# Where a chunked recurrence keeps its decay products, when its inverse begins, and which engine turns the state: a change of order in a fused fp32 kernel

## The chip, the cores and the metric

The kernel runs on one core of one Trainium2 chip. The metric is the device time of one execution in microseconds (us). The core has engines that run side by side and meet at semaphores: TensorE (PE in the profile, its weight loads PEld), VectorE (DVE), ScalarE (ACT), GpSimd (POOL), and a sync engine (SP) that issues most of the DMA transfers; ScalarE issues the others.

## The reference

Two blocks follow each other, all in fp32. The first is a recurrence over 768 tokens for 4 batches of 8 heads, with a state of 40 x 40 per head:

```python
for t in range(S):
    y[:, :, t] = einsum('bhd,bhde->bhe', r_t, state)
    Sa = einsum('bhde,bhe->bhd', state, a_t)
    state = state * w_t[..., None, :] - einsum('bhd,bhe->bhde', Sa, b_t)
    state = state + einsum('bhd,bhe->bhde', v_t, k_t)
```

The second takes the 3072 tokens of 320 channels that come out: `h = x @ w_in` (320 x 2048), `g = h * sigmoid(h)`, `out = g @ w_out` (2048 x 320).

## The kernel before

The 768 tokens are cut into 12 chunks (n = 0 to 11) of 64. Each chunk is handled in two units (m = 0, 1) of two batches. Two chunks, an even and an odd one, make a pair; one inverse serves both, and the second block runs once for a pair. The names that the profile shows are those of the tiles.

**Preparation of a chunk.** `scale` forms the running products W of w along the tokens with a scan on VectorE, and their reciprocals (written over w). GpSimd multiplies a, b and k by them. `scores` multiplies b and a on TensorE (pm), masks the product on VectorE (sb) and sends it to DRAM (md).

```python
def pre(u, md):
    def scale():
        u.W = sb.tile([128, Q, C + 1], F32, name="W", bufs=6)
        R = u.w[:, :, 1 : C + 1]
        ...
        if "pair" in mark and u.n % 2 == 0:
            pin = lambda x: behind(x, mark["row" if u.m == 0 else "across"])
        for be in range(2):
            ...
            pin(nc.vector.tensor_tensor_scan(W, w, one..., 0.0, ALU.mult, ALU.add))
        pin(nc.vector.reciprocal(R, u.W[:, :, 1 : C + 1]))
    ...
    return [scale, scaled, scores, keys] if u.n < 2 else [scale, reciprocals, scaled, rest, scores]
```

`behind(x, y)` only fixes the order: x stands behind y in its engine's queue. `staged(n)` is true for odd chunks above 3: their a is loaded into `stage`, scaled there, and copied into its final tile by `stack`.

**Inverse of a pair.** The masked scores of both chunks come back from DRAM with another layout into the tile `mi` (one buffer). `row` is one multiplication and one reduction on VectorE, each row needs the one before, and there are 31 of them, growing from 1 to 31 x 31 elements per partition. `back` copies the result into mi, from where it goes to DRAM (xd) and returns as XT; `turned` transposes blocks of XT on VectorE, and `first` and `second` merge the blocks with products on TensorE (pq, po).

```python
mark["tiles"] = [sb.tile([128, 2 * SKIP], F32, name="mi"), sb.tile([128, 32 * 32], F32, name="tmp")]
...
def back():
    at = 0
    if N == 32 or hi - lo == 64:
        at = 16
        nc.scalar.copy(out=mi[L, 0:16], in_=turned[L, 0:16])
    x = nc.vector.tensor_copy(out=mi[L, at:32], in_=turned[L, at:32])
    send(queue, xd[L], mi[L])
```

**A chunk's own chain** has six steps: `keys` (transposes pt of b and k), `right` (pr), `solve` (pu, pw with XT), `read` (pl, masked on VectorE into vl), `write` (pgy: the chunk's outputs and the new state GV; VectorE adds, scales by W and forms yx, which ScalarE's queue sends to xs in DRAM), and `turn` (the transposed state GT for the next chunk). For even chunks `turn` is 16 transposes of 32 x 256 on VectorE, for odd ones products with the identity on TensorE (pt<-ident,GV) and copies on ScalarE.

```python
def turn():
    if u.n > 1 and u.n % 2 == 0:
        ... nc.vector.transpose(out=gt[T, :, 32 * e : 32 * e + 32], in_=wide[E, ...]) ...
        return
    ... nc.tensor.matmul(pt..., lhsT=gv[J, j, q], rhs=ident[J, J]) ... nc.scalar.copy(out=gt[R], in_=pt[j][R])
```

**The second block of a pair.** `fetch` brings xs into xt, then 16 steps follow: four `first` (products ph with wi_s and wl_s, activation into gts), four `second` (products po with wo_s), and the same again. They stand in a queue from which `take(k)` puts k steps at the present place of TensorE's order. `weave` mixes two lists of steps evenly.

**The loop over pairs**, for even n from 4 on:

```python
x = prepare(n + 2)
run(merges[1:2] + keys + merges[2:3] + right)
take(1)
run(solve[0:1] + later[0:2] + [x[i] for i in (0, 5, 1, 6) if x])
take(1)
run(solve[1:2] + later[2:3] + [x[i] for i in (2, 7, 3, 8) if x] + read)
take(1)
run([x[i] for i in (4, 9) if x] + write)
each(keyed, n + 1)
take(1)
x = prepare(n + 3)
run([x[i] for i in (0, 2, 5, 7) if x] + turn)
keys, right, solve, read, write, turn = ...              # of chunk n + 1
run(keys + [x[i] for i in (1, 6) if x] + right)
take(1); run(solve[0:1]); take(1)
run(solve[1:2] + [x[i] for i in (4, 9) if x])            # scores of chunk n + 3
rows = invert(n + 3)
run(rows[0:1] + ...); take(1)
x = read + [load vut, take(1)] + write + ...
fetch, more = moe(n, xs)
x += [partial(fetch, 0), partial(queue.extend, more), partial(take, 2)] + turn
weave(x + [partial(take, 1)] * 6, rows[1:36])
```

(The loads are left out here; `merges` and `later` are the steps of the merge.) Chunks 2 and 3 have a passage of their own ahead of the loop, in the same manner.

Of the kernel before, what the change touches and what calls it, by code (L numbers as in the profile page):

```python
# [9 lines left out]
F32 = mybir.dt.float32  # L10
# [31 lines left out]
def kernel(  # L42
# [284 lines left out]
            nc.gpsimd.tensor_copy(out=u.a[J, j], in_=u.stage[J])  # L327

    def pre(u, md):
        def scale():  # L330
            u.W = sb.tile([128, Q, C + 1], F32, name="W", bufs=6)
            R = u.w[:, :, 1 : C + 1]
            pin = partial(in_order, line="vector") if u.n < 2 else lambda x: x
            if "pair" in mark and u.n % 2 == 0:

                pin = lambda x: behind(x, mark["row" if u.m == 0 else "across"])
            for be in range(2):
                W, w = (x[:, P * be : P * be + P].rearrange("p q t -> p (q t)") for x in (u.W, u.w))
                pin(nc.vector.tensor_tensor_scan(W, w, one.rearrange("p q t -> p (q t)"), 0.0, ALU.mult, ALU.add))
            pin(nc.vector.reciprocal(R, u.W[:, :, 1 : C + 1]))  # L340

        def keys():
            R = u.w[:, :, 1 : C + 1]
            nc.gpsimd.tensor_tensor(out=u.kb[:, :, 0], in0=u.kb[:, :, 0], in1=R, op=ALU.mult)
            junk = sb.tile([128, Q, C], mybir.dt.bfloat16, name="junk")
            c = 2 * (NM * u.n + u.m)
            nc.scalar.activation(out=junk, in_=R, func=AF.Square, accum_out=chk[:, c : c + 1])  # L347
            nc.scalar.activation(out=junk, in_=u.W[:, :, 1 : C + 1], func=AF.Square, accum_out=chk[:, c + 1 : c + 2])

        def reciprocals():  # L350
            R = u.w[:, :, 1 : C + 1]
            nc.gpsimd.tensor_tensor(out=u.kb[:, :, 1], in0=u.kb[:, :, 1], in1=R, op=ALU.mult)  # L352

        def rest():
            keys()
            k = NM * u.n + u.m
            for x in [6, 7] if k == 4 else [k + 3]:
                if x < NM * NN:
                    load_w(units[x // NM][x % NM], ([w0] + early)[(x - 4) % 3])

        def scaled():
            if staged(u.n):
                nc.gpsimd.tensor_tensor(out=u.stage, in0=u.stage, in1=u.W[:, :, 0:C], op=ALU.mult)
                return
            for j in range(2):
                J = slice(DP * j, DP * j + DP)
                nc.gpsimd.tensor_tensor(out=u.a[J, j], in0=u.a[J, j], in1=u.W[J, :, 0:C], op=ALU.mult)  # L367
            if u.n < 2:
                R = u.w[:, :, 1 : C + 1]
                nc.gpsimd.tensor_tensor(out=u.kb[:, :, 1], in0=u.kb[:, :, 1], in1=R, op=ALU.mult)  # L370

        def scores():
            if u.m == 0:
                sbs[u.n] = sb.tile([128, NM, 2, P, C], F32, name="sb", bufs=2)
            between(u, sbs[u.n][:, u.m])
            for be in range(2 if u.m == NM - 1 else 0):
                queue = nc.scalar if u.n == 1 or u.n == be == 0 else nc.sync
                for c in range(2):
                    at = 64 * (u.n % 2) + 16 * (2 * be + c)
                    r = C * be + 32 * c  # L380
                    x = send(
                        queue,
                        md[at : at + 16].rearrange("q s t -> s q t"),
                        sbs[u.n][r : r + 32, :, :, :, 32 * c : 32 * c + 32].rearrange("s m j p t -> s (m j p) t"),
                    )
                    if queue is nc.sync:
                        mark["md"] = x.ins
            for x in (4, 5) if u.n == u.m == 1 else ():
                load_w(units[x // NM][x % NM], ([w0] + early)[(x - 4) % 3])

        return [scale, scaled, scores, keys] if u.n < 2 else [scale, reciprocals, scaled, rest, scores]

# [3 lines left out]
    def inverse(md, N, queue, lo=0, hi=128):  # L398
# [38 lines left out]
        def back():  # L437
            turned = XI.rearrange("p t s -> p s t")
            at = 0
            if N == 32 or hi - lo == 64:  # L440
                at = 16
                nc.scalar.copy(out=mi[L, 0:16], in_=turned[L, 0:16])
            x = nc.vector.tensor_copy(out=mi[L, at:32], in_=turned[L, at:32])
            pin(x)
            mark["row"] = x.ins
            send(queue, xd[L], mi[L])
# [163 lines left out]
    def chain(u, xs):  # L610
# [78 lines left out]

        def turn():  # L690

            if u.n > 1 and u.n % 2 == 0:
                wide = GVf[u.m]
                for j in range(2):
                    for e in range(2):
                        for d in range(2):
                            E, T = (slice(DP * j + 32 * x, DP * j + 32 * x + 32) for x in (e, d))
                            at = j * Q * D + 32 * d
                            nc.vector.transpose(
                                out=gt[T, :, 32 * e : 32 * e + 32],  # L700
                                in_=wide[E, at : at + Q * D].rearrange("p (q d) -> p q d", q=Q)[:, :, 0:32],
                            )
                return
            pt = [bank("pt") for _ in range(2)]
            for q in range(Q):
# [203 lines left out]
    def run(steps):  # L909
        for step in steps:  # L910
            step()
# [60 lines left out]
    for u in units[2] + units[3]:  # L972
# [10 lines left out]
    rows = invert(3)  # L983
    weave(
        queue[0:8],
        [x[i] for x in ahead for i in (0, 5, 1, 6, 2, 7, 4, 9, 3, 8)] + [partial(keyed, u) for u in units[2]] + rows[0:19],
        convert[21:31],
    )
    del queue[0:8]
# [29 lines left out]
    take(1)  # L1019
    run(two[0:1] + one_[2:3] + two[1:2] + one_[3:4] + two[2:3] + one_[4:5])  # L1020
    x = prepare(4)
    run(two[3:4] + solve[0:1] + [x[i] for i in (0, 5, 1, 6)] + two[4:5] + solve[1:2] + [x[i] for i in (2, 7, 3, 8)])
    each(keyed, 3)
    run(read)
    each(load_vut, 3)
    take(1)
    run(write + [x[i] for i in (4, 9)])
    each(load_vl, 3)
    x = prepare(5)
    run([x[i] for i in (0, 2, 5, 7)] + turn)  # L1030
    keys, right, solve, read, write, turn = start(3)
    run(keys + [x[i] for i in (1, 6)] + right)
    take(1)
    run(solve[0:1])
    take(1)
    run(solve[1:2] + [x[i] for i in (4, 9)])
    rows = invert(5)
    merges = rows[35:]
    run(rows[0:1] + [x[i] for i in (3, 8)])
    issued["sync"] = mark["mi"]  # L1040
    each(load_v, 4)
    each(load, 6, "bk")
    run(read)
    each(stack, 5)
    x = [partial(each, load_vut, 4), partial(take, 1)]
    x += write + [partial(each, load_vl, 4)] + [partial(keyed, u) for u in units[4]]
    fetch, more = moe(2, xs)
    x += [partial(fetch, 0), partial(queue.extend, more), partial(take, 2)] + turn
    weave(x + [partial(take, 1)] * 8, rows[1:36])
    for n in range(4, NN, 2):  # L1050
        xs = dr.tile([DM, 4 * NM * C], F32, name="xs", bufs=2)
        keys, right, solve, read, write, turn = start(n)
        x = prepare(n + 2)
        later = late.pop(n)
        run(merges[1:2] + keys + merges[2:3] + right)
        each(load_v, n + 1)
        each(load, n + 2, "a")
        each(load, n + 3)
        take(1)
        run(solve[0:1] + later[0:2] + [x[i] for i in (0, 5, 1, 6) if x])  # L1060
        take(1)
        run(solve[1:2] + later[2:3] + [x[i] for i in (2, 7, 3, 8) if x] + read)
        each(load_vut, n + 1)
        take(1)
        run([x[i] for i in (4, 9) if x] + write)
        each(load_vl, n + 1)
        each(keyed, n + 1)
        take(1)
        x = prepare(n + 3)
        run([x[i] for i in (0, 2, 5, 7) if x] + turn)  # L1070
        keys, right, solve, read, write = start(n + 1)[0:5]
        turn = start(n + 1)[5] if n + 2 < NN else []
        run(keys + [x[i] for i in (1, 6) if x] + right)
        each(load_v, n + 2)
        each(load, n + 4, "bk")
        take(1)
        run(solve[0:1])
        take(1)
        run(solve[1:2] + [x[i] for i in (4, 9) if x])
        rows = invert(n + 3)  # L1080
        merges = rows[35:]
        run(rows[0:1] + [x[i] for i in (3, 8) if x])
        take(1)
        if n + 2 < NN:
            each(stack, n + 3)
            x = read + [partial(each, load_vut, n + 2), partial(take, 1)]
            x += write + [partial(each, load_vl, n + 2)] + [partial(keyed, u) for u in units[n + 2]]
            fetch, more = moe(n, xs)
            x += [partial(fetch, 0), partial(queue.extend, more), partial(take, 2)] + turn
            weave(x + [partial(take, 1)] * 6, rows[1:36])  # L1090
        else:
            run(read)
            take(1)
            run(write)
            fetch, more = moe(n, xs)
            fetch(0)
            queue += more
# [155 lines left out]
```

## Time and profile before

| | |
|---|---|
| time, median of 3 | 917.12 us (916.49 to 922.71) |
| span of the profiled execution | 928.1 us |
| TensorE busy | 779.0 us (84%) |
| VectorE busy | 553.2 us (60%) |
| ScalarE busy | 295.8 us (32%) |
| GpSimd busy | 150.9 us (16%) |
| reciprocals of W, VectorE | 24 of 3344 ns |
| turns of GV, VectorE | 80 of 436 ns |
| second block's products ph (wi_s) and po (wo_s), TensorE | 195.8 us and 214.2 us busy |

The page divides the span into 40 equal slices (23.2 us each) and gives the busy share of each engine in tenths; the line PEclk is the clock that TensorE was granted, in tenths of full speed. A group's line names the source line, the engine, the operation, output <- inputs and the shapes, then the busy time and the mean duration of one, then the engine's idle time just before these instructions and what ended most of it. A line of the timeline begins with start and duration in us. Profiled matrix products are counted per pass, two to an fp32 product here. Times in the text without another source are us from the start of the profiled span.

### The profile page before, as it was taken

To read this page: it belongs to the slowest core of one execution; us is meant where nothing else is said; L and a number is where in the kernel's file an instruction comes from. 1 tells how busy PE (TensorE), PEld (TensorE's weight loads), DVE (VectorE), ACT (ScalarE), POOL (GpSimd) and SP (SyncE) were. 2 spreads that over 40 slices of the span, in tenths; PEclk is the share of its full clock that TensorE was granted. 3 is DMA by queue.
4 is the path that set the end of the run, shared out by engine and by line. 5 is a ranking of instruction groups with operands and counts; after the bars stand their busy time and mean duration, and the time that the engine had idled before them with its cause. 6 is when DMAs were issued, how large, how long until landed. Compare 5 with 4: busy or idle time off the path is not lost.

```text
span 928.1 us, 25351 instructions
## 1 busy us (share of the span) xinstructions
PE 779.0 (84%) x10914; PEld 550.9 (59%) x10914; DVE 553.2 (60%) x1084; ACT 295.8 (32%) x688; POOL 150.9 (16%) x156
## 2 busy tenths in 40 slices
PE   2035689998789899999499998599996899996996
PEld 2035587676777557677256767256775366672544
DVE  9989979885376983294973394972577920610000
ACT  2235367543513124231134250125250225220120
POOL 7402033001313101141101140102040000010001
PEclk9665767997599999899799999699998899997999
DMA  7975725654244603537303627212525021212001
GB/s 171 197 145 145 162 75 141 174 140 104 52 87 82 172 2 82 125 67 160 84 23 60 138 65 165 67 43 67 127 57 116 31 46 31 61 23 57 1 1 31
DMA packets 240150, 82.99 MB, mean 89 GB/s; under 512 B 207136, under 2 KB 231968, under 8 KB 240032
## 3 DMA queue, kind: packets, MB, share of 16 engines
q1 hardware_dynamic: 219488, 69.96, 33.8%
q10 hardware_dynamic: 20544, 11.34, 4.8%
q8 instruction: 87, 1.43, 0.6%
q14 instruction: 31, 0.25, 0.1%
HBM read 67.11 MB, written 14.16 MB: 88 GB/s over the span
## 4 chain that ended last, share of the span: by engine, by line
PE 59%; DVE 22%; DMA 10%; issue 3%; ACT 3%; SPq 2%; ACTq 0%; POOLq 0%; DVEq 0%; POOL 0%
PE ph L825 15%; PE po L837 15%; DVE tmp L423 5%; PE pl L268 4%; DVE XI L430 4%; PE ph L830 4%; PE pgy L268 4%; DVE w L340 3%; PE pu L268 3%; PE po L268 3%; PE pt L268 2%; PE pq L268 2%; DMA xs<-yx 2%; PE pr L268 2%; PE pm L268 2%
## 5 line engine op out<-in xcount | busy, mean ns | idle before, releaser
L825 PE MATMUL ph<-xt,wi_s 128*128 128x512 f32 (+1 forms) x448 | 195.8, 584 | 48.1 <-DMA xt<-xs 45.9
L837 PE MATMUL po<-wo_s,gts 128*128 128x320 f32 x768 | 214.2, 436 | 0.0
L837 PEld LDWEIGHTS po<-wo_s,gts 128*128 128x128 f32 x768 | 143.6, 190 | 62.7 <-issue 4.9
L825 PEld LDWEIGHTS ph<-xt,wi_s 128*128 128x128 f32 x448 | 87.7, 206 | 131.8 <-issue 77.3
L832 ACT ACTIVATE gts<-ph 128x512 f32<-128x512 f32 (+1 forms) x112 | 54.3, 534 | 248.8 <-PE ph L830 248.3
L734 DVE TENSOR_TENSOR vl<-pl,ml 128x512 f32<-128x512 f32 x48 | 30.9, 685 | 139.1 <-PE pl L268 81.7
L423 DVE TENSOR_TENSOR tmp<-XI,mi 64x2 f32<-64x2 f32 (+40 forms) x169 | 83.8, 496 | 15.1 <-DMA mi<-md 10.7
L340 DVE RECIPROCAL w<-W 128x512 f32<-128x512 f32 x24 | 80.3, 3344 | 0.9
L430 DVE TENSOR_REDUCE XI<-tmp 64x2 f32<-64x2 f32 (+40 forms) x169 | 76.8, 454 | 4.8
L853 POOL TENSOR_TENSOR ot<-gts,ot 128x320 f32<-128x320 f32 x24 | 20.8, 865 | 282.3 <-ACT gts L851 282.3
L352 POOL TENSOR_TENSOR kb<-kb,w 128x512 f32<-128x512 f32 x20 | 25.3, 1266 | 253.2 <-DVE w L340 157.6
L268 PE MATMUL pm<-a,kb 64*64 64x64 f32 x1280 | 40.1, 235 | 21.9 <-POOL kb L370 15.5
L830 PE MATMUL ph<-xt,wl_s 64*128 64x512 f32 (+1 forms) x224 | 57.9, 594 | 0.0
L268 PE MATMUL pq<-XT,sb 32*32 32x32 f32 (+1 forms) x1280 | 31.0, 207 | 30.8 <-DVE XT L472 15.9
L268 PEld LDWEIGHTS pm<-a,kb 64*64 64x64 f32 x1280 | 36.4, 147 | 27.8 <-POOL kb L370 15.7
L268 PE MATMUL pl<-r,vut 64*128 64x64 f32 x768 | 50.3, 288 | 2.8 <-ACT vl L662 2.3
L268 PEld LDWEIGHTS pl<-r,vut 64*128 64x128 f32 x768 | 48.5, 201 | 5.6 <-ACT vl L662 2.4
L367 POOL TENSOR_TENSOR a<-a,W 64x512 f32<-64x512 f32 x32 | 39.1, 1220 | 66.6 <-PE pq L268 24.0
L347 ACT ACTIVATE junk<-w 128x512 bf16<-128x512 f32 x24 | 15.1, 631 | 105.5 <-DVE w L340 85.0
L268 PEld LDWEIGHTS pq<-XT,sb 32*32 32x32 f32 (+1 forms) x1280 | 27.9, 131 | 35.1 <-issue 18.9
L268 PE MATMUL pt<-ident,kb 128*128 128x128 f32 x192 | 27.9, 304 | 23.4 <-DVE a L312 23.1
L851 ACT COPY gts<-po 128x320 f32<-128x320 f32 x24 | 10.2, 424 | 98.0 <-PE po L837 81.7
(108 smaller groups left out, 1039.9 us busy)
## 6 DMA issues: line engine op xcount, KB each, us to landing
kb<-in_bT SPq DMA_DIRECT2D x48, 128.0 KB
vut<-in_vT SPq DMA_DIRECT2D x48, 128.0 KB
r<-in_rT SPq DMA_DIRECT2D x24, 256.0 KB
w<-in_wT SPq DMA_DIRECT2D x45, 128.0 KB
kb<-in_kT SPq DMA_DIRECT2D x44, 128.0 KB
a<-in_aT SPq DMA_DIRECT2D x32, 128.0 KB
vl<-in_v SPq DMA_DIRECT2D x48, 80.0 KB
xs<-yx ACTq DMA_DIRECT2D x48, 80.0 KB
```

The lines of the kernel that those rows point to most:

```text
L268: x = what(*x, **y)
L340: pin(nc.vector.reciprocal(R, u.W[:, :, 1 : C + 1]))
L352: nc.gpsimd.tensor_tensor(out=u.kb[:, :, 1], in0=u.kb[:, :, 1], in1=R, op=ALU.mult)
L367: nc.gpsimd.tensor_tensor(out=u.a[J, j], in0=u.a[J, j], in1=u.W[J, :, 0:C], op=ALU.mult)
L423: x = nc.vector.tensor_tensor(out=part, in0=X[L, :, t + 1 : N, t + 1 : N], in1=M[L, :, t, t + 1 : N].unsqueeze(2).to_broadcast([hi - lo, I ...
L430: x = nc.vector.tensor_reduce(out=X[L, :, t + 1 : N, t], in_=part, axis=AX.X, op=ALU.add)
L734: nc.vector.tensor_tensor(out=u.vl[:, :, j, D:], in0=pl[j].rearrange("p (q t) -> p q t", q=Q), in1=ml.unsqueeze(1).to_broadcast([128, Q, C ...
L825: in_order(nc.tensor.matmul(ph[n], lhsT=wi_s[:, k, at : at + 128], rhs=xt[:, k, :], start=k == 0, stop=False))
L830: in_order(nc.tensor.matmul(ph[n], lhsT=wl_s[R, i, :], rhs=xt[R, 2, :], start=False, stop=True))
L832: nc.scalar.activation(out=place(2 * i + n)[:, T], in_=ph[n], func=AF.Silu)
L837: in_order(nc.tensor.matmul(po[:, 0:DM], lhsT=place(f)[:, b * 128 : b * 128 + 128], rhs=wo_s[:, NF // 2 * half + f, :], start=f == 0, stop ...
L853: nc.gpsimd.tensor_tensor(out=ot4, in0=rest, in1=ot4, op=ALU.add)
```

## The change

It does four things.

1. The products W of an odd chunk from 5 on are formed in the tile mi, which the inverse does not use at that time, and GpSimd copies them into a W buffer later (`kept`). So the preparation of chunk n + 3 no longer needs a free W buffer and moves ahead of chunk n's `write`.
2. The rows of the inverse stand behind the even chunk's write: the whole chain of the odd chunk, from `keys` on, is now woven with the rows, where before only `read` and `write` were.
3. VectorE turns the state of odd chunks, too (from 5 on); the turn of an odd chunk is held back until the next pair. `back` copies wholly on VectorE.
4. In the passage of chunks 2 and 3 fewer steps of the second block are taken, so that five steps of a pair stand ahead of the next pair's first chunk. Of the other eleven, three come between the odd write and the first step on the next xt, so that TensorE has work while y travels through xs to xt.

```diff
     def pre(u, md):
+        def kept():
+            u.W = sb.tile([128, Q, C + 1], F32, name="W", bufs=6)
+            nc.gpsimd.tensor_copy(out=u.W, in_=u.Wt)
+
         def scale():
-            u.W = sb.tile([128, Q, C + 1], F32, name="W", bufs=6)
+            if staged(u.n):
+                if u.m == 0:
+                    mark["Wt"] = sb.tile([128, 2 * SKIP], F32, name="mi")
+                u.Wt = mark["Wt"][:, Q * (C + 1) * u.m : Q * (C + 1) * (u.m + 1)].rearrange(...)
+            else:
+                u.W = u.Wt = sb.tile([128, Q, C + 1], F32, name="W", bufs=6)
             ...
-            if "pair" in mark and u.n % 2 == 0:
-                pin = lambda x: behind(x, mark["row" if u.m == 0 else "across"])
+            if "pair" in mark:
+                pin = lambda x: behind(x, mark["row" if u.m == u.n % 2 == 0 else "across"])
...
-            if N == 32 or hi - lo == 64:
+            if hi - lo == 64:
                 at = 16
                 nc.scalar.copy(out=mi[L, 0:16], in_=turned[L, 0:16])
...
-            if u.n > 1 and u.n % 2 == 0:
+            if u.n > 1 and u.n != 3:
...  # the loop; the passage before it is changed in the same way and ends with 5 instead of 8 single takes
-        x = prepare(n + 2)
+        x, y = prepare(n + 2), prepare(n + 3)
...
-        run(solve[1:2] + later[2:3] + [x[i] for i in (2, 7, 3, 8) if x] + read)
+        run(solve[1:2] + later[2:3] + [x[i] for i in (2, 8, 3, 9) if x])
+        run([y[i] for i in (0, 6, 1, 7, 2, 8) if y] + held + read)
...
-        run([x[i] for i in (4, 9) if x] + write)
+        run([x[i] for i in (4, 10) if x] + write + [y[i] for i in (5, 11) if y])
         each(load_vl, n + 1)
         each(keyed, n + 1)
         take(1)
-        x = prepare(n + 3)
-        run([x[i] for i in (0, 2, 5, 7) if x] + turn)
-        ...
-        run(keys + [x[i] for i in (1, 6) if x] + right)
-        each(load_v, n + 2)
-        each(load, n + 4, "bk")
-        take(1)
-        run(solve[0:1])
-        take(1)
-        run(solve[1:2] + [x[i] for i in (4, 9) if x])
+        run([y[i] for i in (4, 10) if y])
         rows = invert(n + 3)
-        run(rows[0:1] + [x[i] for i in (3, 8) if x])
-        take(1)
+        run(rows[0:1])
+        run([y[i] for i in (3, 9) if y])
+        x = turn
+        keys, right, solve, read, write = start(n + 1)[0:5]
+        held = start(n + 1)[5] if n + 2 < NN else []
+        x = x + keys + right + [partial(each, load_v, n + 2), partial(each, load, n + 4, "bk")]
+        x += [partial(take, 1), solve[0], partial(take, 1), solve[1], partial(take, 1)]
         if n + 2 < NN:
-            each(stack, n + 3)
-            x = read + [partial(each, load_vut, n + 2), partial(take, 1)]
+            x += [partial(each, stack, n + 3)]
+            x += read + [partial(each, load_vut, n + 2), partial(take, 1)]
             x += write + [partial(each, load_vl, n + 2)] + [partial(keyed, u) for u in units[n + 2]]
             fetch, more = moe(n, xs)
-            x += [partial(fetch, 0), partial(queue.extend, more), partial(take, 2)] + turn
+            x += [partial(fetch, 0), partial(queue.extend, more), partial(take, 2)]
             weave(x + [partial(take, 1)] * 6, rows[1:36])
```

In the order of instructions that results, an even chunk has S S S between its products, then F F F F and one S stand among the odd chunk's, S S S behind the odd write, and F F F F S ahead of the next pair (F and S are the second block's `first` and `second`).

## The prediction

> **What bounds the kernel now.** The second block's work on a pair of chunks comes in two kinds of step: F reads xt (four 128x512 products with wi_s, two with wl_s, two activations), S reads gts (eight products with wo_s). A pair has 8 F and 8 S, in the order F F F F S S S S twice, and from chunk 4 on every pair goes through the same order of work. First view: the page's slices and its groups.
>
> ```profile
> PE   2035689998789899999499998599996899996996
> PEclk9665767997599999899799999699998899997999
> L825 PE MATMUL ph<-xt,wi_s 128*128 128x512 f32 (+1 forms) x448 | 195.8, 584 | 48.1 <-DMA xt<-xs 45.9
> ```
>
> TensorE is busy from the first third on, but a dip comes back every fifth or sixth slice, and PEclk dips with it. The group that waits there is the first F of a pair, for xt: 45.9 us in 5 waits. Second view: the stretch from chunk 6's first merge product (494.6) to chunk 8's (630.6), cut where chunk 7's write ends.
>
> ```profile
> 495.00:574.00 79.00, 77.88 (x1341) 57.28 (x1336) 35.73 (x74) 29.54 (x69) 20.29 (x20) 1.00 0.50 107
> 574.00:630.00 56.00, 43.06 (x251) 24.55 (x246) 47.86 (x79) 10.31 (x20) 2.74 (x2) 0.85 0.27 64
> ```
>
> Columns: stretch, length, busy TensorE, weight loads, VectorE, ScalarE, GpSimd, clock, DMA. In the first stretch TensorE is full and VectorE idles more than half; in the second VectorE is nearly full (the rows of the inverse) and TensorE has a hole and a clock of 0.85. Third view, the order of time, TensorE:
>
> ```profile
> 577.61 1.97 PE L268 MATMUL pm<-a,kb 64*64 64x64 f32 x32 [2.06 <-DVE yx L782]
> 590.46 5.77 PE L825 MATMUL ph<-xt,wi_s 128*128 128x512 f32 x8 [10.88 <-DMA xt<-xs]
> 597.22 3.70 PE L825 MATMUL ph<-xt,wi_s 128*128 128x512 f32 x8
> 601.91 1.98 PE L268 MATMUL pt<-ident,GV 64*40 64x64 f32 x64
> 613.21 17.49 PE L837 MATMUL po<-wo_s,gts 128*128 128x320 f32 x64
> 630.63 1.20 PE L268 MATMUL pq<-XT,sb 32*32 32x32 f32 x64
> ```
>
> (A count of 8 is four products.) Nothing of this pair can be multiplied until both its chunks' y have gone through xs to xt, and nothing of the pair before is left: 10.88 us idle, then the first F at 5.77 for 3.70. VectorE:
>
> ```profile
> 519.02 1.29 DVE L734 TENSOR_TENSOR vl<-pl,ml 128x512 f32<-128x512 f32 x2 [22.67 <-ACT XT L568]
> 571.40 0.16 DVE L423 TENSOR_TENSOR tmp<-XI,mi 128x1 f32<-128x1 f32 x1 [5.36 <-DMA mi<-md]
> 616.77 1.16 DVE L430 TENSOR_REDUCE XI<-tmp 128x31 f32<-128x961 f32 x1
> 624.04 0.70 DVE L472 STREAM_TRANSPOSE XT<-XT 32x512 f32<-32x512 f32 x1 [6.11 <-DMA XT<-xd]
> ```
>
> The rows start at 571.4 and end at 617.9, and XT is turned at 624 to 632, just when TensorE ends its last S (630.6). So both chains close together: filling TensorE alone would bring nothing, the rows have to start earlier too. Why they start so late, the sync queue shows; the scores of chunk 9, which these rows invert, were masked by 557.3:
>
> ```profile
> 555.40 2.05 SPq L221 DMA_DIRECT2D kb<-in_bT  x2
> 562.90 3.18 SPq L221 DMA_DIRECT2D md<-sb  x4
> ```
>
> md is issued behind eight kb loads and two output writes.
>
> **What the skill says.** "TensorE: Matmul & The Clock Gate", What's actually happening: after an idle window of some 3.4 us the array's clock is halved, and is given back after about as long a busy time. The trace agrees (5.77 against 3.70 after 10.88 us idle; 1.00 where TensorE is full). "Perfetto Trace Analysis", Optimization Strategy: where the contended engine changes over time, interleave the regimes. That is this change; the two stretches above are such regimes. "PSUM — Partial Sum Buffer", Engine vs sequencer instructions: ScalarE, VectorE and GpSimd queues are strict FIFO. The trace agrees: VectorE idles 22.67 us before vl with scans of later chunks ready behind it. "VectorE: DVE Perf Modes", The three transpose paths: VectorE turns 32x32 blocks only; here 16 instructions per chunk at 436 ns each.
>
> **The change, part by part.**
>
> *Rows begin behind the even write.* Scans and reciprocals of the odd chunk n+3 move from behind write(n) into VectorE's idle time before vl: 4 scans at 0.74 and 2 reciprocals at 3.34, 9.6 us. With them go the held turn of chunk n-1 (16 x 0.436 = 7.0) and XT's second half: about 18 us into 22.7, so no cost. W has 6 buffers, two a chunk, and chunk n's are read until write(n); hence the products stay in mi and GpSimd copies them to W afterwards (2 copies, an estimate of 1.2 us each from its 128x512 operations at 1.27, beside other work). Now take chunk n's first merge product as t = 0, with durations of this trace: pq, pt, po, pr 7.3; S 4.5; pu/pw and pq 2.9; S 4.5; pu/pw and po 2.9; pl 3.7; S 4.5; pm 2.0; write(n) 5.4 (ends 37.8); pm 2.0; F 4.7; pm of chunk n+3 to t = 46.6. VectorE then has write(n)'s updates, 8.9 from 35.2 (as from 529.3 to 538.2 before), 9 turns (4.0) and the masks, which stand between turns: t = 50. In the sync queue md and mi now follow the vl and r loads, ahead of kb. From the first md issue to mi's landing it took 7.75 before (426.66 to 434.41), so rows start at t = 58. Before it was 571.4 - 494.6 = 76.8: 19 us earlier.
>
> *TensorE's order.* Five steps (F F F F S) of a pair come before the next pair and eleven in it, so that S S S stand between the odd write and the first F. From t = 46.6: pt and pr 3.9, F, pu/pw, F, pu/pw, F, pl 3.7, S: 76; write(n+1) to 81.4; pm 83.4; S S S 13.1 to 96.5. I add 1.8 for pt, whose banks of PSUM are freed by masks that stand behind nine turns: 98.3. Rows: the first 20 take 14.0 (sum of their groups), t = 72; vl at 72 to 75.2; up to row 25 6.7, to 81.9; updates of write(n+1), the last yx at 90. From there to the first F it took 6.4 to 7.8 (715.2 to 721.6; 582.7 to 590.5), so xt is there at t = 97 to 98. TensorE comes at 98.3: the gap closes, with nothing to spare. F F F F S bring 23.2: the next pair starts at 121.5. The last rows end at 90 + 1.4 + 12.5 = 104, copy 1.1, xd and XT 5.0, turned by t = 112: nine us of slack.
>
> *Turns.* 64 products, 1.92 us, leave TensorE in three pairs, and 2.4 us of copies leave ScalarE; VectorE takes 7.0 where it idles.
>
> *Sum.* A pair's work on TensorE without gap: 81.8 (494.6 to 576.4) + 4 x 4.69 + 17.42 = 118.0, and with the 1.8 for pt 119.8; I take 120. Before: from 356.05 to 494.59, 630.63 and 762.76 are 138.5, 136.0 and 132.1. Saved 18.5 + 16.0 + 12.1 = 46.6 us. The start of chunk 4 comes earlier by the three S that now follow chunk 4 instead: there the two small F and two S stand before chunk 3's pl as before, the pm of chunks 4 and 5 have moved ahead, so pl ends near 293.7 (292.0 before), the last yx, now behind row 20, comes at about 308 as before, the first F at 318, and 18.8 + 4.5 + 2 for the slow clock lead to 343 instead of 356. The rows, from about 280 on, are through by 329 and XT by 335, so they don't bind. Those 13.1 us are paid back in the last pair, where they fill its hole: 72.6 up to the last write, S S S 13.1, then 79.6 from the first F to the end at full clock (81.7 less 2.1) and 1 for pt: 166 against 165.3. Total 343 + 3 x 120 + 166 = 869 of the profile's 928.1, a ratio of 0.936; of 917.12 that is 859 us.
>
> **Rivals.** (1) *The gap stays, since xt follows the rows.* The y updates of the odd write stand in VectorE's queue behind row 25. If mi comes late (its buffer is now freed by GpSimd's copies and ScalarE's squares, too), each us puts off xt by a us beyond the one TensorE can cover: 6 us later would mean a pair of 125 and 873 us. For it: the margin of zero above. Against: the copies can start at t = 41, mi lands at 58. (2) *VectorE's added work delays vl or the write of the even chunk.* A scan of mi stands between two vl, waiting for a w load late in the sync queue (I put it at t = 22 to 26, vl at 24). Five us there would be five in each of four pairs: 880. Against it: S and pm still lie between pl and write, 6.5 us. (3) *VectorE becomes the bound.* Its busy time was 83.6 of 135 in a pair; with 7.0 more turns it is 91 of 120. There is slack unless its waits are badly placed; then a pair lasts about 130 and the time is near 890. (4) *Better than thought*: no stall of pt and a clock of 1.00 throughout give 118 a pair, and 852.
>
> **Range and chances.** Most of the gain is work already done at full clock in the first stretch, with a filling that the order of instructions shows; what is unsure is whether waits of 2 to 5 us a pair come in. Predicted 859 us, 8 times in 10 between 847 and 880. Faster by over 2% means under 898.8, so some 40 of the 58 us would have to be lost for it to fail: 0.95. Within 2% 0.04, slower 0.01.
>
> **What the changed profile would show.** The wait of ph for xt falls from 45.9 us to some 10, most of it before chunk 4. pq of chunks 6, 8 and 10 start some 120 us apart, with first rows near t = 58 and clock near 1.00 throughout the pair. Before XT's transposes VectorE idles, or they end well before pq. Turned blocks number 128 and no pt<-ident,GV follows chunk 3. I am wrong if rows start past t = 65, if ph still waits over 5 us in each pair, if vl waits for a scan behind w, or if POOL's copy W<-mi ends after the md issue.

## The result and the profile after

The changed kernel takes 883.09 us (median of 4 runs, 881.11 to 885.63) where the kernel before, run beside it, took 919.09: a ratio of 0.9607, 95% interval 0.9558 to 0.9657. A second comparison gave 0.9626 (0.9597 to 0.9655). Faster, as predicted, but not by as much: 859 was the prediction, 847 to 880 its range.

The page after has a span of 879.6 us instead of 928.1; TensorE is busy 762.4 us of it (87%), VectorE 583.5 (66%). First the slices of TensorE and of its granted clock, and the group that had waited for xt:

```profile
PE   2134688999689999989989989999899999999996
...
PEclk9665868999569999999999999999999999999998
...
L839 PE MATMUL ph<-xt,wi_s 128*128 128x512 f32 (+1 forms) x448 | 185.7, 558 | 6.1 <-ACT gts L846 4.1
```

The dips that came back in every pair are gone, from TensorE and from its clock. Of 45.9 us of waiting for xt nothing is left, and a product takes 558 ns in the mean instead of 584. What remains is 6.1 us, most of it for an activation (gts).

The pairs, from the first pq of chunk 4, 6 and 8 to the next pair's (columns as in the prediction: length, busy TensorE, weight loads, VectorE, ScalarE, GpSimd, clock, DMA):

```profile
340.97:467.35 126.38, 119.75 (x1538) 80.53 (x1537) 98.81 (x164) 39.11 (x90) 27.98 (x26) 0.97 0.42 95
467.35:591.11 123.76, 117.92 (x1538) 79.99 (x1537) 91.22 (x164) 37.29 (x84) 25.87 (x24) 0.99 0.43 97
591.11:712.06 120.95, 118.07 (x1541) 80.48 (x1542) 83.84 (x171) 33.90 (x74) 19.57 (x20) 0.99 0.37 84
```

They were 138.5, 136.0 and 132.1; I had put them at 120 each. Where the second pair's 123.76 us go is seen in the order of time, TensorE first:

```profile
498.47 1.14 PE L268 MATMUL pgy<-r,GT 64*64 64x64 f32 x30 [0.91 <-DVE sb L290]
...
515.61 2.82 PE L268 MATMUL pt<-ident,kb 128*128 128x128 f32 x12 [3.38 <-DVE sb L290]
...
553.30 13.19 PE L851 MATMUL po<-wo_s,gts 128*128 128x320 f32 x48
566.33 3.60 PE L839 MATMUL ph<-xt,wi_s 128*128 128x512 f32 x8
...
578.94 1.98 PE L839 MATMUL ph<-xt,wi_s 128*128 128x512 f32 x4 [1.35 <-ACT gts L846]
...
591.11 1.07 PE L268 MATMUL pq<-XT,sb 32*32 32x32 f32 x56
```

S S S run from 553.30 on, and the first F follows at once at 566.33, taking 3.60 instead of 5.77. The square brackets hold what is left: three waits, of which two are for the masks sb. VectorE's order of the same pair:

```profile
493.60 0.70 DVE L350 TENSOR_TENSOR_SCAN mi<-w,one 128x260 f32<-128x260 f32 x1 [0.56 <-DMA w<-in_wT]
494.22 0.67 DVE L748 TENSOR_TENSOR vl<-pl,ml 128x512 f32<-128x512 f32 x1
494.80 3.34 DVE L351 RECIPROCAL w<-mi 128x512 f32<-128x512 f32 x1
498.06 1.35 DVE L290 TENSOR_TENSOR sb<-pm,ms 128x256 f32<-128x256 f32 x4
...
511.07 4.03 DVE L710 STREAM_TRANSPOSE GT<-GV 32x256 f32<-32x256 f32 x9
515.13 0.76 DVE L290 TENSOR_TENSOR sb<-pm,ms 128x256 f32<-128x256 f32 x2
515.91 0.43 DVE L710 STREAM_TRANSPOSE GT<-GV 32x256 f32<-32x256 f32 x1
516.38 0.76 DVE L290 TENSOR_TENSOR sb<-pm,ms 128x256 f32<-128x256 f32 x2
...
524.32 0.16 DVE L434 TENSOR_TENSOR tmp<-XI,mi 128x1 f32<-128x1 f32 x1 [4.90 <-DMA mi<-md]
...
539.38 1.29 DVE L748 TENSOR_TENSOR vl<-pl,ml 128x512 f32<-128x512 f32 x2 [2.07 <-PE pl L268]
...
577.07 0.70 DVE L483 STREAM_TRANSPOSE XT<-XT 32x512 f32<-32x512 f32 x1 [0.18 <-DMA XT<-xd]
```

A reciprocal of 3.34 us stands right ahead of the first masks, and nine transposes, 4.03 us, right ahead of the second. The rows start at 524.32, 57.0 us into the pair (76.8 before), and the first blocks of XT are turned at 577, 14 us ahead of pq. The masks also hold up the sync queue, whose order is:

```profile
508.85 0.40 SPq L221 DMA_DIRECT2D r<-in_rT  x1
517.16 2.06 SPq L221 DMA_DIRECT2D md<-sb  x4
519.32 2.12 SPq L221 DMA_DIRECT2D mi<-md  x2
```

md goes out as the last mask ends (516.38 + 0.76); the kb loads no longer stand ahead of it.

### The profile page after: what moved, and what is told of

The parts are those of the page before. It is cut to its first block, busy times and chain, and to the rows that moved or that the text cites. A ratio compares the mean times of both kernels' runs of the same rounds, so it can differ in the third digit from the quotient of the medians.

```text
span 879.6 us, 24987 instructions
## 1 busy us (share of the span) xinstructions
PE 762.4 (87%) x10722; PEld 541.6 (62%) x10722; DVE 583.5 (66%) x1132; ACT 286.3 (33%) x672; POOL 159.3 (18%) x164
## 4 chain that ended last, share of the span: by engine, by line
PE 50%; DVE 33%; DMA 7%; issue 3%; SPq 2%; ACT 2%; POOL 1%; ACTq 0%; POOLq 0%; DVEq 0%
PE ph L839 14%; PE po L851 12%; DVE tmp L434 6%; DVE XI L441 5%; DVE w L351 5%; PE ph L844 4%; PE pl L268 3%; PE pt L268 3%; PE po L268 3%; PE pgy L268 2%; SPq L221 2%; PE pr L268 2%; PE pq L268 2%; PE pu L268 2%; DVE GV L787 2%
## 5 line engine op out<-in xcount | busy, mean ns | idle before, releaser
L839 PE MATMUL ph<-xt,wi_s 128*128 128x512 f32 (+1 forms) x448 | 185.7, 558 | 6.1 <-ACT gts L846 4.1
L839 PEld LDWEIGHTS ph<-xt,wi_s 128*128 128x128 f32 x448 | 83.7, 196 | 86.4 <-issue 66.2
L434 DVE TENSOR_TENSOR tmp<-XI,mi 64x2 f32<-64x2 f32 (+40 forms) x169 | 84.6, 501 | 23.6 <-DMA mi<-md 18.7
L867 POOL TENSOR_TENSOR ot<-gts,ot 128x320 f32<-128x320 f32 x24 | 24.4, 1018 | 328.8 <-ACT gts L865 325.4
L441 DVE TENSOR_REDUCE XI<-tmp 64x2 f32<-64x2 f32 (+40 forms) x169 | 76.8, 455 | 5.1
L710 DVE STREAM_TRANSPOSE GT<-GV 32x256 f32<-32x256 f32 x128 | 55.7, 435 | 28.8 <-DMA GV<-in_v 26.9
L268 PE MATMUL pm<-a,kb 64*64 64x64 f32 x1280 | 40.8, 239 | 18.7 <-POOL kb L381 15.5
L351 DVE RECIPROCAL w<-W 128x512 f32<-128x512 f32 x16 | 53.5, 3343 | 0.5
```

The source lines that it names most:

```text
L268: x = what(*x, **y)
L351: pin(nc.vector.reciprocal(R, u.Wt[:, :, 1 : C + 1]))
L434: x = nc.vector.tensor_tensor(out=part, in0=X[L, :, t + 1 : N, t + 1 : N], in1=M[L, :, t, t + 1 : N].unsqueeze(2).to_broadcast([hi - lo, I ...
L441: x = nc.vector.tensor_reduce(out=X[L, :, t + 1 : N, t], in_=part, axis=AX.X, op=ALU.add)
L710: x = nc.vector.transpose(out=gt[T, :, 32 * e : 32 * e + 32], in_=wide[E, at : at + Q * D].rearrange("p (q d) -> p q d", q=Q)[:, :, 0:32],)
L839: in_order(nc.tensor.matmul(ph[n], lhsT=wi_s[:, k, at : at + 128], rhs=xt[:, k, :], start=k == 0, stop=False))
```

## The experiments

**Theory.** The change works as meant, and needs both of its parts; what the prediction missed are waits in in-order queues (masks behind nine turns or a reciprocal, an activation behind a square), each with some clock lost behind it, and a scale taken from one long execution of the kernel before. **Rivals.** The filling with S S S gives nearly all of it; the early rows do; VectorE has become the bound, so that a wait removed comes back elsewhere; the masks' place doesn't matter.

**The kernel before again.** No edit.

> The kernel before, unchanged, profiled once more. The first profile of it has a span of 928.1 us, while its timed runs were 916.5 to 922.7 us. Theory A: the extra 8 to 11 us belong to that one execution; then this profile spans 916 to 921 us, and its pairs of chunks (first pq to first pq) are shorter than 138.5, 136.0 and 132.1 us by some 2 to 3 us each. Theory B: the profile lengthens this kernel each time; then it spans 926 to 930 us with the same pairs, and the ratio that I took to 928.1 was no mistake.

A span of 918.0 us, with pairs of 135.96, 134.74 and 132.73, and chunk 4 starting at 350.04 instead of 356.05. So theory A for the span; of the 10.1 us, 6.0 lie ahead of chunk 4, 3.3 in the pairs and 0.8 in the tail, where I had expected most of it in the pairs. The timed runs of the kernel before went from 916 to 931 us over the comparisons, so the profile of 928.1 shows a long execution; profiling does not lengthen this kernel each time.

**The shift of steps alone** (in the kernel before, the passage ahead of chunk 4):

```diff
-    weave(x + [partial(take, 1)] * 8, rows[1:36])
+    weave(x + [partial(take, 1)] * 5, rows[1:36])
```

> The kernel before with one part of the change alone: five steps ahead of chunk 4, so that S S S stand behind the odd write; rows of the inverse, turns and scans stay where they were. Theory 1 (both chains ended together, so filling TensorE's hole alone brings nothing a pair): pairs of chunks 4, 6 and 8 still last 132 to 137 us, ph's wait for xt nearly vanishes, but the wait of pq for XT (the turned inverse) grows to 8 to 13 us a pair; time 905 to 920 us, that is 0 to 14 below before. Rival (the filling is the gain, the rows hardly matter): pairs 122 to 127 us and 880 to 890 us in all, as the full change.

906.89 us, ratio 0.9832 (0.9783 to 0.9880); pairs of 130.2, 129.1 and 124.3. TensorE's order, from the start of one pair to that of the next:

```profile
479.36 0.31 PE L268 MATMUL pq<-XT,sb 32*32 32x32 f32 x2 [3.42 <-DVE XT L472]
480.50 1.91 PE L268 MATMUL pq<-XT,sb 32*32 32x32 f32 x62 [0.83 <-DVE XT L472]
...
578.34 3.60 PE L825 MATMUL ph<-xt,wi_s 128*128 128x512 f32 x8
...
603.36 1.34 PE L837 MATMUL po<-wo_s,gts 128*128 128x320 f32 x4 [2.87 <-ACT gts L832]
608.43 0.31 PE L268 MATMUL pq<-XT,sb 32*32 32x32 f32 x2 [3.73 <-DVE XT L472]
```

The hole ahead of F is filled, and TensorE now waits for the rows' result XT and for gts, 7 to 8 us a pair (22.8 us for XT in all, 13.0 of them at the start of chunk 4; a pair waits some 4.3 us for XT, where theory 1 had 8 to 13). The time is in theory 1's range, the pairs 2 to 8 us below it: the filling alone does bring something, 6 to 8 us a pair against the second profile of before. In the kernel before the first blocks of XT were turned at 624.0 and 624.9, and pq ran at 630.6: the rows' chain had 5 to 6 us of slack, and that is what this edit takes.

**The rows alone** (the changed kernel, with eight single steps ahead of chunk 4 instead of five: rows early, turns on VectorE, but no S between the odd write and F):

```diff
-    weave(x + [partial(take, 1)] * 5, rows[1:36])
+    weave(x + [partial(take, 1)] * 8, rows[1:36])
```

> The changed kernel with eight steps ahead of chunk 4, as before: rows of the inverse early and turns on VectorE, but no S between the odd write and the first F of a pair. Theory 1: the hole of about 11 us and the slow first F (+2 us) come back in every pair, less what the turns no longer take of TensorE (1.9 us in each of three pairs) and less the wait for XT; pairs 130 to 134 us, ph waits for xt 9 to 12 us a pair, time 898 to 912 us. Rival (the early rows alone give the gain, since xt also comes earlier): ph waits under 4 us a pair, pairs 122 to 127, time 880 to 890 us.

933.03 us, ratio 1.0115 (1.0079 to 1.0150), 1.2% slower than the kernel before and outside both expectations; pairs of 135.3, 136.6 and 136.5. In the second pair TensorE waits 11.12 for xt, 2.39 for the odd write's yx, 2.55 + 0.16 for the masks and 1.31 for an issue, 17.5 us; in the kernel before (the second profile) it was 10.83 + 3.32 + 0.42 = 14.6. So the hole is as long as ever, the early rows don't shorten the way of y to xt, and the new order adds the waits for the masks. Of the 9.7 us by which this profile (927.7) exceeds the second one of before, 5.0 lie in the pairs, 3.7 ahead of chunk 4 and 0.9 in the tail.

**The turns behind the masks** (the changed kernel; `masked` is the last mask of the scores of a chunk kept in mi):

```diff
             if u.n < 2:
                 in_order(x, "vector")
+            if staged(u.n):
+                mark["masked"] = x.ins
...
                             if u.n % 2 == 1:
                                 behind(x, mark["across"])
+                            elif "masked" in mark:
+                                behind(x, mark["masked"])
```

> The changed kernel with one order of VectorE's queue altered: the 16 transposes of the even chunk's GV stand behind the four masks of chunk n+3's scores instead of nine of them ahead. Theory 1 (pt waits for its PSUM banks since nine transposes stand before the masks): the waits of pt for the masks, 8.5 us in three pairs, and with them most of ph's wait for gts vanish, md is issued some 3 to 4 us earlier and the first row runs at t = 53 to 55 instead of 57; time 6 to 9 us below the changed kernel, 874 to 877 us. Rival (VectorE is the bound, a wait saved in one place comes back in the next): pairs stay within 1 us of 126.4, 123.8 and 120.9 and the time at 882 to 884 us.

865.72 us, ratio 0.9386 (0.9353 to 0.9419): 17 us below the changed kernel, twice what was expected. Its stretches and its VectorE:

```profile
340.48:458.35 117.87, 116.27 (x1538) 78.78 (x1537) 96.64 (x160) 38.90 (x90) 28.94 (x26) 1.00 0.46 102
458.35:576.21 117.86, 116.27 (x1538) 78.77 (x1537) 92.59 (x168) 37.04 (x84) 25.91 (x24) 1.00 0.46 102
```

```profile
501.29 1.42 DVE L290 TENSOR_TENSOR sb<-pm,ms 128x256 f32<-128x256 f32 x4 [1.25 <-PE pm L268]
502.62 7.21 DVE L712 STREAM_TRANSPOSE GT<-GV 32x256 f32<-32x256 f32 x16
510.38 0.16 DVE L436 TENSOR_TENSOR tmp<-XI,mi 128x1 f32<-128x1 f32 x1 [0.54 <-DMA mi<-md]
```

The masks now wait for their products, not the other way round, and the sixteen turns lie in the time in which mi travels: 0.54 us of idleness where 4.90 were. The rows start at 52.0 us of the pair, pt never waits, and the clock is 1.00 in the first two pairs (0.97 in the third). The pairs are shorter by 8.5, 5.9 and 0.7 us, while the waits of pt in them had been 2.57, 3.38 and 2.55. In the first pair the other waits go too (1.08 for the masks ahead of pgy, 2.79 for gts, of which 1.4 stay), and TensorE's work takes 116.27 us instead of 119.75, the clock being 1.00 instead of 0.97. Over the three pairs TensorE is idle for 3.9 us instead of 15.2, and busy for 3.6 us less: the 15 us gained are waits and clock. VectorE has 92 to 97 us of work in 118, so it still idles; whether it is the bound, the odd turns below decide.

**The square behind the activation** (ScalarE's square of an even chunk's 1/W, which waits for a late reciprocal, put behind the activation emitted last):

```diff
-            nc.scalar.activation(out=junk, in_=R, func=AF.Square, accum_out=chk[:, c : c + 1])
+            x = nc.scalar.activation(out=junk, in_=R, func=AF.Square, accum_out=chk[:, c : c + 1])
+            if u.n > 5 and u.n % 2 == 0:
+                behind(x, mark["silu"])
```

> The changed kernel with one order of ScalarE's queue altered: the square of 1/W of chunk n+2, which waits for a late reciprocal, stands behind the activation of the F in hand instead of ahead of it. Theory 1 (waits in the in-order queues are what the prediction missed, each also costing clock): ph's waits for gts, 4.1 us in two pairs, vanish, and with the 0.83 clock at the end of pair 4 the time falls by 3 to 5 us, to 878 to 881 us where the changed kernel has 883. Rival (only the masks matter; a wait at the pair's end is covered by what follows): within 1 us of the changed kernel.

882.69 us, ratio 0.9564 (0.9502 to 0.9626): nothing beyond the scatter, the rival's result. The waits for gts did go, but the pairs are 123.5, 125.9 and 123.3, 1.7 us longer in sum. The clock took it: over the three pairs TensorE is idle for 3.4 us less, but busy for 5.1 us more. The second pair, the stretch with the wait of pt (3.38 and 3.39 us) and the one after it, of the changed kernel and of this one:

```profile
507.00:517.00 10.00, 6.62 (x85) 3.90 (x84) 8.97 (x20) 2.52 (x6) 0.62 (x1) 0.91 0.24 64
517.00:527.00 10.00, 10.00 (x148) 6.54 (x147) 4.59 (x19) 4.09 (x9) 2.44 (x4) 0.92 0.69 142
```

```profile
506.60:516.60 10.00, 6.61 (x84) 3.62 (x83) 8.96 (x20) 2.28 (x5) 0.62 (x1) 0.91 0.31 74
516.60:526.60 10.00, 10.00 (x80) 7.08 (x80) 4.10 (x15) 2.61 (x5) 2.44 (x4) 0.57 0.72 137
```

The same wait is followed, in the stretch after it, once by a clock of 0.92 and once by 0.57 (80 products in it instead of 148): 0.8 or 4.3 us of full clock lost. So while the wait of pt is there, a microsecond saved behind it can't be read from the total.

**Both orders.** The two edits together.

> Both orders altered: even chunk's turns behind the masks, and the square behind the activation. The kernel with the turns behind the masks took 865.7 us, with ph still waiting 2.7 us for gts in two pairs. Theory 1: those waits go, 1 to 3 us less, 863 to 865 us, pairs 116.5, 116.5 and 118 to 120 us. Rival: no further gain, 865 to 866 us.

864.76 us, ratio 0.9389 (0.9326 to 0.9452). The waits for gts are gone and the pairs take 117.0, 116.7 and 116.8 us, within 0.5 us of what was expected in the first two and better in the third; but chunk 4 started 3.7 us later (344.15), in the passage that the edit doesn't touch, and the total can't be told from the turns behind the masks alone.

**The odd turns back on TensorE** (in the kernel with the turns behind the masks):

```diff
-            if u.n > 1 and u.n != 3:
+            if u.n > 1 and u.n % 2 == 0:
```

> The kernel with the even turns behind the masks, and the turns of chunks 5, 7 and 9 given back to TensorE and ScalarE (64 products of 64x64 each) as before the change. Theory 1 (TensorE is the bound, VectorE turns lie in idle time): 1.9 us more in each of three pairs, pairs of 119.8, 119.8 and 122 us, 871 to 873 us in all where all turns on VectorE gave 865.7. Rival (VectorE, 93 to 97 us busy of 118, is or is near the bound): same or faster, 862 to 866 us.

873.75 us, ratio 0.9497 (0.9431 to 0.9563), 8 us above the same kernel with all turns on VectorE; the profiles differ by 6.3 (869.8 and 863.5), where theory 1 has 5.8, but 1.5 of the 6.3 lie ahead of chunk 4, which the edit doesn't touch. The pairs are 118.0, 120.7 and 118.8 and the tail grows from 167.1 to 170.3: the held turns of chunks 5, 7 and 9 fall into the pair after, so the second and the tail pay (2.8 and 3.3), and the first does not, which the expectation had wrong. In the third the clock hides it: 0.97 in the kernel compared with, 1.00 here; against that kernel's second profile, with a clock of 1.00 (116.2, below), it pays 2.6. The rival, VectorE as the bound, falls.

**The rows alone, masks ahead.** The rows alone, and the turns behind the masks.

> The kernel with eight steps ahead of chunk 4 (no S behind the odd write) and early rows, which took 933 us, with the turns put behind the masks as well. Theory 1 (early rows alone lose because nine transposes stand before the masks, as in the changed kernel, while the hole of 11 us stays): the pt waits of 8.1 us go, pairs fall from 135 to 137 us to 130 to 133 us, time 912 to 920 us, so a little below before (919 to 925 us). Rival (early rows lose because rows stand before the odd write's y in VectorE's queue and put off xt): pairs 133 to 136 us and 925 us or more.

923.17 us, ratio 0.9992 (0.9967 to 1.0016), pairs of 133.8, 133.9 and 133.3: no different from before.

```profile
573.24 1.97 PE L268 MATMUL pm<-a,kb 64*64 64x64 f32 x32 [2.34 <-DVE yx L800]
585.45 6.02 PE L843 MATMUL ph<-xt,wi_s 128*128 128x512 f32 x8 [10.24 <-DMA xt<-xs]
...
606.53 17.49 PE L855 MATMUL po<-wo_s,gts 128*128 128x320 f32 x64
```

The waits for the masks are gone, as theory 1 has it, worth 1.2% against before; the pairs lie where the rival put them, since the wait for the odd write's yx and the hole of 10 us with the slow F behind it stay, and the time lies between the two expectations. Early rows without S S S bring nothing, even well ordered: no product waits for XT, and with the hole in it TensorE's own chain alone takes 133 to 134 us. That makes four combinations, relative to before: neither part 1, the filling 0.983, the rows 1.012, both 0.961; and with the masks ahead of the turns, the rows 0.999, both 0.939.

**The changed kernel again, the masks again, and a third order.** On one chip, side by side: the changed kernel; the turns behind the masks; and both orders with, besides, this in the passage ahead of chunk 4, which takes the scans and the reciprocal of (5, m1) from between chunk 3's masks:

```diff
-    run([y[i] for i in (0, 6, 1, 7, 2, 8)])
+    run([y[i] for i in (0, 1, 2)])
     each(keyed, 3)
+    run([y[i] for i in (6, 7, 8)])
```

> The changed kernel, unchanged, timed beside the next two on one chip, since the kernel before moved from 919 to 926 us between chips. Theory 1: 882 to 887 us, pairs of 123 to 127, 123 to 126 and 120 to 124 us, a ratio of 0.955 to 0.965 to before. If waits of pt near 3.4 us sometimes slow TensorE's clock and sometimes not, the pairs differ from 126.4, 123.8 and 120.9 by up to 4 us either way, with the same waits.

887.05 us, ratio 0.9626 (0.9597 to 0.9655); pairs of 125.2, 123.5 and 124.5, with pt waiting 8.5 us again. The third is 3.5 us longer than the first time.

> The kernel with the even turns behind the masks, unchanged, on the same chip. Theory 1: 864 to 868 us, pairs 116.5 to 118 us (chunk 8's 117 to 121), 16 to 20 us under the changed kernel. If the gain had been the chip's and not the order's, it would lie within 5 us of the changed kernel.

868.34 us, ratio 0.9423 (0.9395 to 0.9451): 18.7 us below the changed kernel on the same chip. The pairs are 120.2, 119.1 and 116.2 us, the first two longer than expected: waits for gts (2.67 and 1.37 us) and for the masks ahead of pgy (1.01 and 1.25) came back in them, though at a clock of 1.00. In sum the pairs take 355.6 us, against 356.0 the first time and 373.1 in the changed kernel beside it.

> Both orders altered, and in the passage before chunk 4 the scans and reciprocal of (5, m1) stand behind chunk 3's masks instead of between them. Theory 1 (a wait removed from TensorE's path is worth itself and up to as much again in clock): the wait of pl for a, 3.7 to 4.2 us once, goes, chunk 4 starts at 336 to 340 us instead of 340.5 to 344, and the time is 859 to 862 us. Rival (that passage is bound by VectorE's rows or by XT, so the reciprocal's 3.4 us come back before chunk 4): start and time unchanged, 863 to 866 us.

861.41 us, ratio 0.9353 (0.9312 to 0.9395). The wait of pl for a is gone, chunk 4 starts at 338.2 instead of 342.0, and the pairs take 117.0, 118.2 and 117.5. By medians that is 6.9 us below the turns behind the masks and 25.6 below the changed kernel; the former is at the edge of what these runs can tell (the intervals meet at 0.9395), the latter is clear. The profiles differ by 6.6, 3.8 of them ahead of chunk 4 and 2.8 in the pairs, where the square's order may have a part. It has the lowest ratio here. Of theory 1's sizes the start holds; more clock than the wait itself was not gained.

Not tried: more buffers of W, which would spare the detour through mi.

## Why the prediction missed

**What held.** The hole closes: F doesn't wait. That it starts 99.0 us into the pair (predicted 98.3) is luck, for two errors cancel: with the turns behind the masks it starts at 93.1, so my walk along TensorE's order (96.5 without the 1.8 for pt) was 3.4 us too long, and 1.8 was too little for waits and clock, which took 5.9. That there is nothing to spare isn't shown. The rows start at 57.0 (58), the second masks end at 49.8 (50), XT's first blocks are turned by 111.7 (112). GpSimd's copies take 0.62 us each (1.2 estimated from its products) and end at 510.3, before md's issue at 517.2. 128 turned blocks, none on TensorE after chunk 3. So rival 1 (xt follows the rows) and rival 3 (VectorE the bound) didn't come, and the clock was 0.97 to 0.99 rather than 1.00. Of rival 2 a small form did: in the second pair one unit's scans were done ahead of vl; the other's stood between the even chunk's last two vl and waited for w, 0.29 and 0.56 us, so the last vl ran behind a scan that waited for w (494.22), one of the signs of being wrong that I had named. The reciprocal came behind them, and TensorE waited 0.91 us for the masks ahead of pgy.

**The first step that failed: "I add 1.8 for pt".** Against the predicted total of 869 us in the profile stand 879.6: start 341 for 343, pairs 371.1 for 360, tail 167.5 for 166. It is the pairs: they were 8.4, 5.8 and 2.9 us longer than the 118.0 us that I called work without gap, where 1.8 (rounded to 2) was allowed. In the second pair the masks came as early as I had them, but TensorE was ready for pt at 44.9 us and not at 46.6, so pt waited 3.38; then 0.91 for the masks ahead of pgy, 1.35 for gts and 0.19 for yx, none of them in my sum. The 118.0 was itself 1.7 too long, 1.1 of that being waits in the stretch it was taken from: with the turns behind the masks TensorE is busy for 116.3 us of the first two pairs, at a clock of 1.00 in both profiles, and the pairs of 117.87 and 117.86 hold 1.6 us of waits. (My own walk came to 121.5, not 120: the two disagreed by the same 1.7.) From 116.3, the changed kernel's pairs are 6.6 + 3.5, 5.8 + 1.7 and 2.7 + 1.7 us longer, waits and slower work: 22 us in three pairs, of which 1.8 a pair was foreseen and another 1.7 was covered by chance. So the step was mis-sized: waits in queues and slower work cost 10.1, 7.5 and 4.4 us, and I had 1.8. I had seen the nine turns ahead of the masks and counted them as 1.8 us, instead of asking who waits for the masks and at what clock work resumes. The profile of before held the answer to the second, in front of the line at 577.61 that I showed:

```profile
574.40 1.15 PE L268 MATMUL pm<-a,kb 64*64 64x64 f32 x32
```

These 32 products take 1.15 us; the next 32, of the same shape, take 1.97 after a wait of 2.06 us, at a clock of 0.50, ahead of the hole of 10.88. And scans of chunk 9 did not stand ready behind vl through VectorE's 22.67 us, as I wrote: their w loads were issued only from 516.74 on. What a queue's order does shows in the changed kernel, where the products of the second masks ended at 511.64 and the masks ran at 515.13, behind nine transposes.

**The second: "a ratio of 0.936; of 917.12 that is 859".** 928.1 was one execution some 10 us longer than the timed ones (918.0 in a second profile), so the ratio set a long execution's length against the median of others. The changed kernel's own profile is 3.5 us shorter than its timed median; with that, 869 would have been 872.5. The miss of 24.1 us is thus 13.5 from the scale and 10.6 from the sum. Either alone would have left the result inside the range.

**A third, which cost nothing here: "filling TensorE alone would bring nothing".** It brought 1.7%. The rows' result was there 5 to 6 us before pq, and the last two transposes at 630.4, which I read as the end of that chain, are not what pq waits for. The early rows alone brought nothing, or a loss. The gain of both together, 3.9%, is more than the sum of 1.7% and −1.2%, and this joint effect was the core of the prediction and holds.

## What to carry over

Where two chains end together, look for the last consumer of each before saying what one of them alone is worth, and test each part alone and both together: here one part alone gave 1.7%, the other a loss, both 3.9%. Cheap work moved into an engine's idle time is free only by its place in the queue: the same sixteen transposes behind the four masks instead of nine ahead of them were worth 17 to 19 us, about half of what the whole change brought. When a prediction goes from a profile to a time, take the scale from a profile whose length agrees with the timed runs.

## What was not expected of the hardware

TensorE's clock after a short wait. The Trainium skill, "TensorE: Matmul & The Clock Gate", What's actually happening, speaks of an idle window of some 3.4 us; here waits shorter than that were followed by a lower clock as well, but not each time. Over the 10 us after waits of 2.5 to 2.7 us the clock was 0.66 (the first pair with the square moved), 0.83 (the first pair of the changed kernel) and 1.00 (all three pairs of the rows alone; the first pair of the second profile with the turns behind the masks). After 3.38 and 3.39 us it was 0.85 and 0.53. After waits of 0.8 to 1.4 us with no longer one close by, in the three pairs of every kernel here, it was 1.00 each time. And in the third pair with the turns behind the masks the clock was 0.71 over 10 us, with only 0.49 us of idleness recorded in them. What decides it these runs don't show; some records of products may be missing from a trace. The practical reading, for these kernels, is that a wait of 2 to 3.4 us on TensorE costs itself and 0 to some 5 us more, and that totals of kernels with such waits scatter by that much a pair.
